# Attention, gated MLP and slot MLP in one kernel: the sums' 1e-9 as a second column, sink values split by a cast and one operation, and a set-up called later

## Chip, core and metric

The kernel runs on one core of a Trainium2 chip. The metric is device time in microseconds of one execution, launch to end. The parts of a core that matter here are TensorE (PE in the profile; PEld is its weight load), VectorE (DVE), ScalarE (ACT), GpSimd (POOL) and the queue on SyncE (SP) that issues all DMAs.

## Reference

Three layers, all in fp32, follow one another. Attention has 4 batches, 8 heads, 768 positions and 64 dimensions per head; a query sees the 4 first keys (the sinks) and the 128 keys up to itself.

```
scores = np.where(keep, scores, -1000000000.0)
scores = scores - np.max(scores, axis=-1, keepdims=True)
a = np.exp(scores)
a = a / (np.sum(a, axis=-1, keepdims=True) + 1e-09)
attn = np.matmul(a, v)                               # -> x, 3072 x 512
gate = 1.0 / (1.0 + np.exp(-(x @ w_gate)))
x = (gate * (x @ w_val)) @ w_out                     # d_ff = 1536
logits = x @ phi                                     # 8 experts x 4 slots = 32
d = softmax over the tokens; slot_input = d.T @ x
slot_out[e] = np.maximum(slot_input[e] @ w1[e], 0.0) @ w2[e]
out = softmax over the slots of logits @ slot_out    # 3072 x 512
```

## The kernel before

The 3072 tokens are worked in 8 halves of a batch (384 tokens each). A half has 4 pairs of heads, and a pair has 3 units of 128 queries, so there are 96 units. `stage_a` of a unit makes the scores on PE (L300, two heads), masks them and takes the row minimum of their negative on DVE (L304), and exponentiates on ACT (L321), which also writes the sum of each row to a column of the tile `sm` (128 x 2, one column per head). The inner function `norm` adds 1e-9 to the sums (L325), takes the reciprocal (L326), and has POOL multiply the probabilities (L327). `stage_b` transposes them on PE, `stage_c` multiplies them with the values; `sink_parts` (L339, L340) splits the sinks' probabilities into a high and a low part. Some products take a value as such a pair of parts.

`sinks(b)` does such a split for the sinks' values of batch b, once for each of the 4 batches: the tile `rv` is loaded, and `cut` makes from it, in four DVE operations on 128 x 512 elements, the tile `vs`, which holds the high part in the rows where `vsel[:, 0:1]` is 1 and the low part in the others:

```
pin(dve.tensor_copy(vh, rv))
dve.tensor_tensor(rv, rv, vh.bitcast(F32), op=ALU.subtract)
dve.tensor_scalar(rv, rv, vsel[:, 1:2], None, op0=ALU.mult)
dve.scalar_tensor_tensor(vs, vh.bitcast(F32), vsel[:, 0:1], rv, op0=ALU.mult, op1=ALU.add)
```

The MLP's weights come as 64-bit floats. In the first of five passes over them, `w_start` makes fp32 of each of 36 tiles: two operations on ACT (L513, L514), three on DVE (L517, L518, L521), one on POOL (L525), and a DMA writes it out for the later passes. `gemm1` (L632) multiplies with gate and value weights, `gemm2` (L670) with the output weights, and DVE adds the latter's result into `ysb` (L675). The first half's attention comes before the first MLP product; the attention of later halves is spread between the products, by a credit that the main loop keeps. `setup_merge` fills constants (`ones`, `R`, `dm`, `R2`) that only the end of the kernel reads.

All engines take their instructions in order. The order is not the order of the code alone: a scheduler sets it when the program is built, and only instructions under `pin` keep the code's order among themselves.

Of the kernel before, what the change touches and what calls it, by code (L numbers as in the profile page):

```python
# [9 lines left out]
F32 = mybir.dt.float32  # L10
# [5 lines left out]
ALU = mybir.AluOpType  # L16
AX = mybir.AxisListType
# [19 lines left out]
def fused_kernel(ctx, tc, qT, kA, kB, vB, vS, wg, wv, wo, phi, w1, w2, n_sink, window, out):  # L37
    nc = tc.nc
    pe, act, dve, pool, sp = nc.tensor, nc.scalar, nc.vector, nc.gpsimd, nc.sync
# [8 lines left out]
    def ps(tag, bufs, dt=F32):  # L48
        return psum.tile([128, 512], dt, name=tag, tag=tag, bufs=bufs)
# [13 lines left out]
    pin = tc.keep_in_program_order  # L63

    def setup_masks(cp):
# [34 lines left out]
        pin(dve.tensor_copy(identr, ident))  # L100

        pin(dve.tensor_reduce(vsel[:, 0:1], ident.rearrange("p (a b) -> p a b", b=16)[:, :, 0:8], axis=AX.XY, op=ALU.max))
        pin(dve.tensor_scalar(vsel[:, 1:2], vsel[:, 0:1], -1.0, 1.0, op0=ALU.mult, op1=ALU.add))
        for t in T2 + tt2:
            pool.memset(t.bitcast(F32), 0.0)

# [14 lines left out]
    vsel = per.tile([128, 2], F32, name="vsel")  # L121
# [38 lines left out]
    at = left.enter_context(tc.tile_pool(name="at", bufs=1))  # L160
# [8 lines left out]
    def later(k, fn):  # L169
        pend.append([k, fn])  # L170
# [72 lines left out]
    def run_split():  # L243
        at_tasks.popleft()[1]()
# [3 lines left out]
    def sinks(b):  # L248

        rv = at.tile([128, 4, 128], F32, name="rv", tag="rv", bufs=1)  # L250
        sp.dma_start(out=rv, in_=vS[:, 4 * b:4 * b + 4])

        def cut():
            vh = at.tile([128, 4, 128], F32R, name="vh", tag="vh", bufs=1)
            vs = at.tile([128, 4, 128], F32R, name="vs", tag="vs", bufs=2)
            pin(dve.tensor_copy(vh, rv))
            dve.tensor_tensor(rv, rv, vh.bitcast(F32), op=ALU.subtract)
            dve.tensor_scalar(rv, rv, vsel[:, 1:2], None, op0=ALU.mult)
            dve.scalar_tensor_tensor(vs, vh.bitcast(F32), vsel[:, 0:1], rv, op0=ALU.mult, op1=ALU.add)
            VS[b] = vs  # L260
        later(3, cut)

# [11 lines left out]
    def stage_a(u):  # L274
# [18 lines left out]
        else:  # L293
            P = at.tile([128, 2, 260], F32, name="P", tag="P", bufs=3)
        nb = at.tile([128, 2], F32, name="nb", tag="nb", bufs=4)
        sm = at.tile([128, 2], F32, name="sm", tag="sm", bufs=4)
        Ss = [ps("ys", 3) for h in range(2)]
        for i, k in enumerate(QK[n][1:]):
            for h in range(2):
# [19 lines left out]
            src, dst = P[:, :, 0:128], PC[n][:, jj, :, 4:132]  # L319
        for h in range(2):  # L320
            act.activation(out=dst[:, h], in_=src[:, h], func=ACTF.Exp, scale=-1.0,  # L321
                           bias=nb[:, h:h + 1], accum_out=sm[:, h:h + 1])

        def norm():
            dve.tensor_scalar(sm, sm, 1.0e-9, None, op0=ALU.add)  # L325
            dve.reciprocal(sm, sm)  # L326
            pool.tensor_tensor(dst, dst, sm.unsqueeze(2).to_broadcast([128, 2, src.shape[2]]), op=ALU.mult)  # L327
            if wide:
                act.copy(PC[n][:, jj, :, 0:4], P[:, :, sk:sk + 4])
            normed.add(u)  # L330
            if jj == 2:
                later(1, sink_parts)
# [263 lines left out]
    ops = [(si, o, i) for si in range(NS) for o, i in (LAST if si == NS - 1 else ORDER[len(steps[si][0]) - 1])]  # L596
    LA = 4
    w_due, due = {}, {}
    for k, (si, o, i) in enumerate(ops):
        ns, h = steps[si]  # L600
# [424 lines left out]
    fast = nc.values_load(flag, min_val=0, max_val=1)  # L1025
    phase[0] = 0

    setup_merge()
    credit = 0.0
    NX = [10, 5, 8]  # L1030
    xe = []
# [1 line left out]
    for k, (si, o, i) in enumerate(ops):  # L1033
        phase[0] = steps[si][0][0] // NF
        if o == "y":
            if si:
                gemm2(si - 1, i)
        else:
            gemm1(si, i, o)
        tick()  # L1040
        now[0] = k + 1
        rate = 0.0
        for h in range(NH):
            todo = half_at[h] - emitted[0] - credit
            if todo > 0 and due[h] > now[0]:
                rate = max(rate, todo / max(due[h] - (3 if h == 1 else 5) - now[0], 1))
        credit += rate
        while credit >= 1:
            credit -= 1
            attn_piece()  # L1050
        if m2:
            m2_piece()
            if si == NS - 1:
                m2_piece()
        if x_can():
            x_split()
        if at_tasks:
            run_split()
        w_slot()
        if not xe and len(tops) == 1 and ws_n[0] >= 3 * NF and not w_fly:  # L1060
            top.close()
            tops.append(top.enter_context(tc.tile_pool(name="parts", bufs=1)))
        if not xe and not pieces and xs_n[0] == NH:
            top.close()
            left.close()
            xe.append(ctx2.enter_context(tc.tile_pool(name="xe0", bufs=1, reuse_waits="tile")))
        if len(xe) == 1 and min(gdone[0], ydone[0]) >= N_LEAN - 1 and m2_done[0] == NH - 1:
            inner.close()
            xe.append(ctx2.enter_context(tc.tile_pool(name="xe1", bufs=1, reuse_waits="tile")))
        for q in range(len(xe)):  # L1070
            if 32 - len(e_order) in range(sum(NX[0:q]), sum(NX[0:q + 1])):
                e_load(e_tile(xe[q], f"e{q}", NX[q]))
                break
# [68 lines left out]
```

## Time and profile before

| | |
|---|---|
| median of 3 runs | 944.0 us (943.19 to 945.39) |
| the profiled execution | 944.22 us |
| its span, first to last instruction | 942.3 us |
| busy: PE | 898.0 us (95%) |
| busy: DVE | 598.7 us (64%) |
| busy: POOL | 475.9 us (51%) |
| busy: ACT | 372.4 us (40%) |
| mean granted clock of TensorE | 0.972 |

The profile is one execution; 1.9 us of its time lie outside its span. A share of busy time is a mean over stages that differ: what an engine does while another waits for it has to be read stage by stage. Busy time of one DVE instruction includes what it is held up after its start, and two that follow each other closely overlap by some 0.08 us in the records.

### The profile page before, as it was taken

Reading aid. Unit: us, or ns where it says so; the run is one execution under the profiler, and the core shown is the slowest. Engines: PE = TensorE matmul, PEld = TensorE weight load, DVE = VectorE, ACT = ScalarE, POOL = GpSimd, SP = SyncE. Lnnn points to the kernel's source line nnn. Section 1 sums busy time; section 2 is a strip of 40 time slices with the busy share of each in tenths; the row PEclk is TensorE's granted clock in tenths of the full one; section 3 lists DMA queues with packets and bytes.
Section 4 is the critical chain, followed back from the end, with each engine's and each line's share of the span. In section 5 each row is a group of like instructions: output and inputs, shape, how many; then the busy total and the mean of one; then the engine's idle time right before and its main releaser. Section 6 shows DMA issues by size and latency. Waiting matters only on the chain.

```text
span 942.3 us, 15253 instructions
## 1 busy us (share of the span) xinstructions
PE 898.0 (95%) x5276; PEld 712.5 (76%) x5277; DVE 598.7 (64%) x1536; ACT 372.4 (40%) x996; POOL 475.9 (51%) x428
## 2 busy tenths in 40 slices
PE   8789998989999999999999999999999999899894
PEld 4455554556789999888889999898999987798452
DVE  8996869666558757765776767766455533444532
ACT  5675565333343343344343443343332323241221
POOL 3753445463346675655675756654644422684000
PEclk7799999999999999999999999999999999999897
DMA  6884657531213232333232333231212169656997
GB/s 230 285 268 154 226 173 230 165 100 44 68 54 103 82 106 54 106 84 99 59 105 68 98 78 96 77 101 55 79 57 68 45 211 387 230 155 196 310 323 236
DMA packets 80355, 133.40 MB, mean 142 GB/s; under 512 B 6800, under 2 KB 38544, under 8 KB 80272
## 3 DMA queue, kind: packets, MB, share of 16 engines
q1 hardware_dynamic: 80272, 132.37, 46.1%
q8 instruction: 43, 0.70, 0.3%
q14 instruction: 40, 0.33, 0.1%
HBM read 116.62 MB, written 15.73 MB: 140 GB/s over the span
## 4 chain that ended last, share of the span: by engine, by line
PE 78%; DVE 8%; DMA 4%; issue 4%; ACT 3%; POOL 1%; SPq 0%; POOLq 0%; DVEq 0%; ACTq 0%
PE gv L632 39%; PE ys L670 20%; PE ys L300 4%; PE xt L392 4%; DMA wraw<-wsv 2%; PE ys L857 2%; PE pt L367 2%; DVE wA L517 2%; DVE wA L518 1%; PE ys L697 1%; PE xt L395 1%; PE ys L706 1%; DVE wA L521 1%; PE xt L878 1%; DMA wbits<-in_wv_dram 1%
## 5 line engine op out<-in xcount | busy, mean ns | idle before, releaser
L632 PE MATMUL gv<-xh,whv 128*128 128x384 f32 x432 | 151.6, 379 | 3.2 <-ACT whv L190 3.2
L632 PE MATMUL gv<-xh,whg 128*128 128x384 f32 x432 | 153.1, 383 | 0.0
L670 PE MATMUL ys<-who,gh 128*128 128x512 f32 x324 | 140.2, 460 | 7.8 <-DVE ysb L675 6.3
L649 POOL TENSOR_TENSOR gl<-th,gh 128x384 fp32r<-128x384 f32 x84 | 89.3, 1063 | 111.8 <-DVE gh L192 95.0
L675 DVE SCALAR_TENSOR_TENSOR ysb<-ys,ysb 128x512 f32<-128x512 f32 x138 | 93.0, 683 | 37.8 <-PE ys L670 37.1
L632 PE MATMUL gv<-xh,wlv 128*128 128x384 f32 x336 | 114.3, 340 | 0.7 <-POOL wlv L495 0.7
L632 PE MATMUL gv<-xl,whv 128*128 128x384 f32 x336 | 114.3, 340 | 0.0
L632 PE MATMUL gv<-xl,whg 128*128 128x384 f32 x336 | 114.0, 339 | 0.0
L632 PE MATMUL gv<-xh,wlg 128*128 128x384 f32 x336 | 113.3, 337 | 0.0
L321 ACT ACTIVATE PC<-P,nb 128x132 f32<-128x132 f32 (+1 forms) x152 | 60.2, 397 | 109.0 <-DVE P L315 77.7
L670 PE MATMUL ys<-wlo,gh 128*128 128x512 f32 x252 | 99.5, 395 | 0.0
L670 PE MATMUL ys<-who,gl 128*128 128x512 f32 x252 | 98.4, 396 | 0.0
L632 PEld LDWEIGHTS gv<-xh,whv 128*128 128x128 f32 x432 | 81.3, 190 | 20.0 <-issue 6.4
L327 POOL TENSOR_TENSOR PC<-PC,sm 128x264 f32<-128x264 f32 (+1 forms) x76 | 50.3, 663 | 90.4 <-DVE sm L326 68.3
L632 PEld LDWEIGHTS gv<-xh,whg 128*128 128x128 f32 x432 | 81.7, 191 | 16.0 <-issue 4.7
L495 POOL TENSOR_TENSOR wlv<-wraw,whv 128x512 fp32r<-128x512 f32 x48 | 63.0, 1313 | 58.6 <-ACT whv L190 54.0
L670 PEld LDWEIGHTS ys<-who,gh 128*128 128x128 f32 x324 | 60.2, 189 | 36.6 <-issue 18.2
L645 DVE SCALAR_TENSOR_TENSOR th<-th,gv 128x384 f32<-128x384 f32 x84 | 46.3, 551 | 61.4 <-PE gv L632 50.5
L495 POOL TENSOR_TENSOR wlg<-wraw,whg 128x512 fp32r<-128x512 f32 x48 | 62.5, 1302 | 34.1 <-ACT whg L190 26.9
L304 DVE CUSTOM_DVE_ANT_0 P<-ys,mask 128x260 f32<-128x260 f32 (+1 forms) x152 | 57.2, 392 | 34.1 <-PE ys L300 34.0
L636 ACT ACTIVATE th<-gv 128x384 f32<-128x384 f32 x96 | 46.8, 487 | 80.4 <-PE gv L632 79.8
L325 DVE TENSOR_SCALAR sm<-sm 128x2 f32<-128x2 f32 x96 | 35.9, 374 | 63.5 <-ACT PC L321 57.9
(211 smaller groups left out, 1834.7 us busy)
## 6 DMA issues: line engine op xcount, KB each, us to landing
ew<-in_w_dram SPq DMA_DIRECT2D x32, 1024.0 KB, 12.1
wraw<-wsg SPq DMA_DIRECT2D x48, 256.0 KB, 2.7
wraw<-wsv SPq DMA_DIRECT2D x48, 256.0 KB, 2.7
wraw<-wso SPq DMA_DIRECT2D x48, 256.0 KB, 2.7
wbits<-in_wg_dram SPq DMA_DIRECT2D x12, 512.0 KB, 4.2
wbits<-in_wv_dram SPq DMA_DIRECT2D x12, 512.0 KB, 4.6
wbits<-in_wo_dram SPq DMA_DIRECT2D x12, 512.0 KB, 4.7
out_dram<-ew SPq DMA_DIRECT2D x8, 768.0 KB, 6.8
```

Of the source, the lines that this page charges most:

```text
L300: pe.matmul(Ss[h][:, 0:w], QK[n][0][h][:, 128 * jj:128 * jj + 128], k[h][:, w0:w0 + w], start=(i == 0), stop=(i == len(QK[n]) - 2))
L304: dve.tensor_tensor_reduce(out=P[:, h, 0:w], in0=S[:, 0:w], in1=mask[:, MOFF[mt]:MOFF[mt] + w], scale=-0.125, scalar=3.0e38, op0=ALU.add, ...
L321: act.activation(out=dst[:, h], in_=src[:, h], func=ACTF.Exp, scale=-1.0, bias=nb[:, h:h + 1], accum_out=sm[:, h:h + 1])
L327: pool.tensor_tensor(dst, dst, sm.unsqueeze(2).to_broadcast([128, 2, src.shape[2]]), op=ALU.mult)
L392: pe.matmul(xt[64 * h:64 * h + 64, cols], VT[n][:, jj + s - i, 64 * h:64 * h + 64], pts[:, i, h, :], start=(jj == 0 and i == 0), stop=Fals ...
L495: pool.tensor_tensor(lo, r, hi.bitcast(F32), op=ALU.subtract)
L632: pe.matmul(acc_ps[:, 0:384], wt[:, 128 * d:128 * d + 128], xt[:, d, :], start=(k == 0), stop=(k == 4 * len(seq) - 1))
L636: act.activation(out=th, in_=acc_ps[:, 0:384], func=ACTF.Tanh, scale=0.5)
L645: dve.scalar_tensor_tensor(gr, th, 1.0, acc_ps[:, 0:384], op0=ALU.add, op1=ALU.mult)
L649: pool.tensor_tensor(gl, gr, gh.bitcast(F32), op=ALU.subtract)
L670: pe.matmul(yp, a[:, 128 * i:128 * i + 128], w, start=(k == 0), stop=(k == len(seq) * len(ns) - 1))
L675: dve.scalar_tensor_tensor(ysb[h][:, i, :], yp, 0.5, ysb[h][:, i, :], op0=ALU.mult, op1=ALU.add)
```

## The change

Four places change. The exponentials' sums go to the first column of a new tile `sm2` (128 x 2 x 2), whose second column is set to 1e-9 by a memset; `norm` adds the two columns by one reduce in place of an addition of a constant. `cut` makes the high part by a cast on ACT and `vs` by one DVE operation, `vh * (vsel0 - 1) + rv`; `vsel[:, 1:2]` becomes `vsel0 - 1`. The call of `setup_merge` moves from ahead of the main loop to a quarter of the way through it.

```
-        pin(dve.tensor_scalar(vsel[:, 1:2], vsel[:, 0:1], -1.0, 1.0, op0=ALU.mult, op1=ALU.add))
+        pin(dve.tensor_scalar(vsel[:, 1:2], vsel[:, 0:1], -1.0, None, op0=ALU.add))
...
-            pin(dve.tensor_copy(vh, rv))
-            dve.tensor_tensor(rv, rv, vh.bitcast(F32), op=ALU.subtract)
-            dve.tensor_scalar(rv, rv, vsel[:, 1:2], None, op0=ALU.mult)
-            dve.scalar_tensor_tensor(vs, vh.bitcast(F32), vsel[:, 0:1], rv, op0=ALU.mult, op1=ALU.add)
+            act.copy(vh, rv)
+            dve.scalar_tensor_tensor(vs, vh.bitcast(F32), vsel[:, 1:2], rv, op0=ALU.mult, op1=ALU.add)
...
+        sm2 = at.tile([128, 2, 2], F32, name="sm2", tag="sm2", bufs=4)
         sm = at.tile([128, 2], F32, name="sm", tag="sm", bufs=4)
+        dve.memset(sm2[:, :, 1:2], 1.0e-9)
...
-                           bias=nb[:, h:h + 1], accum_out=sm[:, h:h + 1])
+                           bias=nb[:, h:h + 1], accum_out=sm2[:, h, 0:1])
...
-            dve.tensor_scalar(sm, sm, 1.0e-9, None, op0=ALU.add)
+            dve.tensor_reduce(sm, sm2, axis=AX.X, op=ALU.add)
             dve.reciprocal(sm, sm)
...
-    setup_merge()
...
+        if k == len(ops) // 4:
+            setup_merge()
```

The scheduler orders the changed program anew. Three places follow. From `norm` on, the changed program's lines have numbers one higher (the reduce is L326, the reciprocal L327); `sm_221`, `sm_358` and the like are buffers of `sm2`.

**First place.** DVE soon after the start, in the first units' masks (L304, a row for the operation and a row `nb` for its accumulator), where the first batch's `cut` stands; before:

```order
L256 CAST vh<-rv 128x512
L326 RECIPROCAL sm<-sm 128x2
L517 TENSOR_SCALAR wA<-wA 128x512
L304 ISA PW,nb<-ys,mask 128x260
L304 ISA nb 128x1
L257 TENSOR_TENSOR rv<-rv,vh 128x512
L304 ISA PW,nb<-ys,mask 128x260
L304 ISA nb 128x1
L518 TENSOR_SCALAR wA<-wA 128x512
L325 TENSOR_SCALAR sm<-sm 128x2
```

The same stretch of DVE in the changed program:

```order
L326 TENSOR_REDUCE sm<-sm_221 128x2
L103 TENSOR_SCALAR vsel<-vsel 128x1
L305 ISA PW,nb<-ys,mask 128x260
L305 ISA nb 128x1
L327 RECIPROCAL sm<-sm 128x2
L257 SCALAR_TENSOR_TENSOR vs<-vh,vsel,rv 128x512
L297 MEMSET sm_358 128x2
L305 ISA PW,nb<-ys,mask 128x260
L305 ISA nb 128x1
L305 ISA P,nb<-ys,mask 128x128
```

Three of `cut`'s four operations are gone, the last one stands before the first weight's L517 (now L518), and each reciprocal is followed by the memset of a later unit's `sm2`. Four such memsets stand at the program's start. `cut` of the second batch, which stood far behind (second place), now stands 48 rows below this one.

ACT, a little later in the first half, where that second batch's cast now stands between exponentials (L322), weights (L514, L515) and copies of transposed probabilities (L363):

```order
L330 COPY PC<-PW 128x2x4
L363 COPY pts<-pt 128x512
L322 ACTIVATE PW,sm_393<-PW,nb 128x260 x2
L515 ACTIVATE wS<-wbits 128x512
L256 CAST vh<-rv 128x512
L330 COPY PC<-PW 128x2x4
L363 COPY pts<-pt 128x512
```

The first batch's cast is ACT's first instruction after its warm-up, ahead of all exponentials; the third's stands 19 rows below the second's; the last one comes later.

**Second place.** DVE in the first pass over the weights, between two additions into `ysb` (L675 before, L676 in the changed program); before, with the second batch's `cut`:

```order
L675 SCALAR_TENSOR_TENSOR ysb<-ys,ysb 128x512
L256 CAST vh<-rv 128x512
L518 TENSOR_SCALAR wA<-wA 128x512
L325 TENSOR_SCALAR sm<-sm 128x2
L257 TENSOR_TENSOR rv<-rv,vh 128x512
L521 SCALAR_TENSOR_TENSOR wA<-wbits,wA 128x512
L326 RECIPROCAL sm<-sm 128x2
L258 TENSOR_SCALAR rv<-rv,vsel 128x512
L517 TENSOR_SCALAR wA<-wA 128x512
L259 SCALAR_TENSOR_TENSOR vs<-vh,vsel,rv 128x512
L518 TENSOR_SCALAR wA<-wA 128x512
L304 ISA P,nb<-ys,mask 128x260
```

And in the changed program:

```order
L676 SCALAR_TENSOR_TENSOR ysb<-ys,ysb 128x512
L522 SCALAR_TENSOR_TENSOR wA<-wbits,wA 128x512
L518 TENSOR_SCALAR wA<-wA 128x512
L326 TENSOR_REDUCE sm<-sm_1412 128x2
L519 TENSOR_SCALAR wA<-wA 128x512
L327 RECIPROCAL sm<-sm 128x2
L297 MEMSET sm_1671 128x2
L522 SCALAR_TENSOR_TENSOR wA<-wbits,wA 128x512
L518 TENSOR_SCALAR wA<-wA 128x512
L519 TENSOR_SCALAR wA<-wA 128x512
L305 ISA P,nb<-ys,mask 128x260
```

All four operations of `cut` have left this place. The next addition into `ysb` follows 19 rows below the first before, and 16 rows below it in the changed program, with seven operations on weights between the two in both. The third batch's one operation stands 23 rows behind that next addition.

**Third place.** DVE at the start, where the scheduler had put `setup_merge` (L134, L135, L142) among the masks; before:

```order
L134 TENSOR_TENSOR R<-ident 96x32
L142 COPY R_77<-ident 128x16
L88 SCALAR_TENSOR_TENSOR mask<-cid,nwf,mask 128x128
L142 COPY R_77<-ident 128x16 x3
L118 TENSOR_REDUCE flm<-fl 128x1
L135 TENSOR_TENSOR R<-R,ident 96x32
L142 COPY R_77<-ident 128x16 x4
```

And in the changed program:

```order
L134 TENSOR_TENSOR R<-ident 96x32
L142 COPY R_77<-ident 128x16
L88 SCALAR_TENSOR_TENSOR mask<-cid,nwf,mask 128x128
L142 COPY R_77<-ident 128x16 x3
L118 TENSOR_REDUCE flm<-fl 128x1
L135 TENSOR_TENSOR R<-R,ident 96x32
L142 COPY R_77<-ident 128x16 x4
```

Nothing moved here, though the call stands elsewhere in the code: these instructions depend on little, and the scheduler takes them as early as before.

## Rows read from the trace of the kernel before

**Rows 1.** Windows: stretch, length, busy (x count) of PE, PEld, DVE, ACT, POOL; clock; DMA.
```profile
0.00:70.00 70.00, 57.60 (x253) 32.32 (x255) 62.70 (x206) 46.10 (x136) 37.37 (x42) 0.80 0.80 261
70.00:200.00 130.00, 122.92 (x511) 67.30 (x510) 96.97 (x230) 67.35 (x176) 62.05 (x53) 0.99 0.59 181
200.00:780.00 580.00, 580.00 (x3544) 510.04 (x3545) 374.48 (x962) 216.04 (x599) 324.00 (x291) 1.00 0.30 85
```

**Rows 2.** Waits of PE, 0 to 70 us: total, times, longest.
```profile
PE ys L300 <- DVE nb L304: 6.1, 7, 1.6
```

**Rows 3.** Waits of PE, 70 to 200 us.
```profile
PE ys L670 <- DVE ysb L675: 6.3, 3, 2.8
```

**Rows 4.** Chain that ended last, 0 to 70 us: shares, then start, length, piece.
```profile
by line: DVE wA L517 13.5%; issue 8.7%; DVE wA L518 8.2%; DVE PW L304 6.3%; ACT PW L321 6.0%; DVE wA L521 5.8%; DVE sm L325 5.5%; DMA nw<-in_window_dram 5.1%; DMA rv<-in_vS_dram 3.4%; PE gv L632 3.0%; PE ys L300 2.9%; DVE Ta L340 2.0%; ACT 
...
12.23 0.34 DVE vh L256
...
13.31 1.11 DVE rv L257
...
15.57 0.40 DVE rv L258
```

**Rows 5.** Timeline of DVE, first 7 us: start, length, instruction, idle before it.
```profile
0.83 0.06 DVE L108 MEMSET m_run<- 96x2 f32 x1
...
4.84 0.17 DVE L79 CAST nwt<-nw 128x4 f32<-128x4 int32 x1 [2.47 <-DMA nw<-in_window_dram]
...
6.62 0.15 DVE L118 TENSOR_REDUCE flm<-fl 128x1 f32<-128x4 f32 x1
```

**Rows 6.** Windows of L325 alone: its busy time and count.
```profile
0.00:66.00 66.00, 7.12 (x15) 0.79 0.81 266
```

**Rows 7.** Timeline of DVE, 26 to 42 us.
```profile
26.79 1.01 DVE L325 TENSOR_SCALAR sm<-sm 128x2 f32<-128x2 f32 x1
27.71 0.68 DVE L521 SCALAR_TENSOR_TENSOR wA<-wbits,wA 128x512 int32<-128x512 int32 x1
...
30.28 1.10 DVE L325 TENSOR_SCALAR sm<-sm 128x2 f32<-128x2 f32 x1 [0.52 <-ACT PW L321]
...
31.49 1.15 DVE L517 TENSOR_SCALAR wA<-wA 128x512 f32<-128x512 f32 x1
```

**Rows 8.** Timeline of POOL, the same stretch.
```profile
30.07 1.28 POOL L525 TENSOR_TENSOR whg<-wA,wS 128x512 int32<-128x512 int32 x1
```

**Rows 9.** Line 517 and line 325: ns min/median/max.
```profile
L517 DVE TENSOR_SCALAR wA<-wA x36: 399/427/1521, 12.6 to 169.3; 128x512 f32<-128x512 f32 x36
L325 DVE TENSOR_SCALAR sm<-sm x96: 155/170/1781, 10.5 to 735.9; 128x2 f32<-128x2 f32 x96
```

**Rows 10.** Tile rv, first 13 us: issue on SP (length; start), time to landing.
```profile
L251 SPq DMA_DIRECT2D rv<-in_vS_dram x1: 432/432/432, 3.5 to 3.5; - x1
...
DMA to landing us min/median/max: 4.3/4.3/4.3
```

**Rows 11.** Timeline of ACT, 8 to 12 us.
```profile
9.01 0.40 ACT L321 ACTIVATE PC<-P,nb 128x128 f32<-128x128 f32 x1 [6.78 <-DVE nb L304]
...
11.31 0.66 ACT L513 ACTIVATE wA<-wbits 128x512 f32<-128x512 f32 x1
```

**Rows 12.** Chain that ended last, 136 to 150 us.
```profile
138.13 1.10 DVE vh L256
...
140.73 0.59 DVE rv L257
...
142.00 0.38 DVE rv L258
...
142.72 0.07 DVE vs L259
142.80 1.53 issue
```

**Rows 13.** Timeline of PE, 136 to 152 us.
```profile
149.36 1.98 PE L670 MATMUL ys<-who,gh 128*128 128x512 f32 x4 [2.40 <-DVE ysb L675]
```

## The prediction

> **What bounds the kernel now.** I read the windows first. From 200 to 780 us PE is busy for all of 580.00 us, and no other engine for more than two thirds; from 0 to 70 us PE is busy for 57.60 us and DVE for 62.70 us, from 70 to 200 us PE for 122.92 us [rows 1]. So PE lies idle for 12.4 us in the first stretch and 7.1 us in the second, 19.5 us in all, and only what shortens these idle times shortens the kernel, because the work of PE itself is not touched by the change. The waits say whom PE waits for: first mostly DVE's masking, which sets the scores' buffers free [rows 2], later DVE's addition into `ysb`, three times and 6.3 us [rows 3]. The chain of the first 70 us runs mostly through DVE: the weights' L517, L518 and L521, the masks and, with 5.5% (3.9 us), L325, an addition on 128 x 2 elements [rows 4]. Work taken off DVE there should let PE start its full stretch earlier, by as much as the chain gets shorter.
>
> Every unit beyond 200 us has the same edits, and I cost them at nothing: PE's own work covers them, with DVE busy for 374.48 of 580 us. Were that cover gone, they would cost or bring what the same edits do early on. After 780 us no L325 is left (the last begins at 735.9 [rows 9]), and the fourth batch's `cut` comes long before that.
>
> **Part 1, the sums.** L325 took 0.17 us at the median and up to 1.78 us [rows 9]. In the first 66 us fifteen of them took 7.12 us [rows 6]; at 0.16 us each that is 2.4, so 4.7 us are time in which they were held. The rows show by what: one began at 30.28 us and took 1.10, to 31.38, and POOL's instruction that began at 30.07 and took 1.28 ended at 31.35 [rows 7, 8]. The reduce that takes its place is nearest to the row of a reduce from 4 elements to one, 0.15 us [rows 5], so without a hold it costs the same, and the question is what of the 4.7 us goes. The bounds are 0 and all of it. What speaks for little: the held L325 at 26.79 us is followed by L521 [rows 7], which would have met the same POOL instruction, as far as L521 is held too. What speaks for something: behind the one at 30.28 us, L517 was held as well (1.15 us, against a median of 0.43) [rows 7, 9]. Without the first hold L517 meets the POOL instruction that held L325, and the second hold, 0.7 us, goes. With L517, L518 and L521 making up 27.5% of the chain [rows 4], the next instruction that can be held is seldom far. I take a third, **-1.5 us**.
>
> The Trainium skill, SBUF — State Buffer (Who interferes with whom), says that DVE and GpSimd share one pair of ports, that a copy, cast or addition of a constant between SBUF tiles can hold it against GpSimd or be held, and that a reduce never contends. The row at 30.28 us agrees with the first half; no row here shows a reduce beside a busy POOL. By that rule alone the reduce is never held and the sum would be -4.7 here; the rule itself leaves open whether the next instruction is held in its stead.
>
> Against this stand 96 memsets. By the order, twenty come before the first half's attention is done, about the first 66 us. Four stand at the program's start, ahead of L79, before which DVE idles for 2.47 us until a DMA lands [rows 5]; they are hidden there. The other sixteen cost 0.06 us each by the nearest row, a memset of 96 x 2 [rows 5]: **+1.0 us**. From below the bound is 0 (they fall into idle gaps); from above it is that they are held as L325 was, 7.12 / 15 = 0.47 us each, +7.6 in all. I take the memset's own row, which ran with POOL hardly started and is all there is. No exponential waits for them: a memset follows the reciprocal of the unit four before, well ahead of its unit.
>
> **Part 2, `cut`.** For the first batch three DVE operations go: 0.34, 1.11 and 0.40 us on the chain [rows 4], 1.85 in all. The fourth keeps its size. But the order brings the second batch's one operation into the first half: 0.60 us when nothing holds it (L521 is the same kind and size, 0.68 less 0.08 of overlap [rows 7]), up to 1.60 as its forerunner needed later (0.07 and 1.53) [rows 12]; the middle is 1.1. Together **-0.75 us**, between -1.25 and -0.25.
>
> The cast goes to ACT. The first stands ahead of all exponentials. Its data were issued at 3.5 us and landed 4.3 us later, so at 7.8 to 7.9 us, and ACT idled before its first exponential at 9.01 us [rows 10, 11]; the cast, 0.66 us by the nearest row [rows 11], fits between. If the data came 1.2 us later, the exponentials behind it and all that follows them would wait. The second and third casts fall into ACT's busy stretch, 46.10 of 70 us [rows 1]: 0 if beside other work, 1.3 us if both lie on the chain. ACT's exponentials hold 6.0% of that chain [rows 4], so most of it is covered; I take **+0.3 us**. The loads of `rv` are issued earlier on SP for the second and third batch, and what is queued behind them there are weight loads and stores; they wait for one DVE operation each, which now comes early, so I add nothing.
>
> Later, at the second place, four operations leave DVE: 1.10, 0.59, 0.38 and 1.60 us on the chain, 3.67 in all [rows 12]. They stand right ahead of the 2.40 us for which PE waited for the addition into `ysb` [rows 13]. Two of them were plainly held, and holds may move on to their neighbours: unheld they are 0.34, 0.59, 0.38 and 0.60, or 1.9 us. A little later the third batch's one operation comes in, 0.6 to 1.6 us, before the last of the three waits. So DVE gains between 0.3 and 3.1 us by then; the middle, **-1.7 us**. What is late next is the same addition, at its two other waits (3.9 us together by rows 3 and 13), which shrink no further when a DMA or PE itself sets them.
>
> **Part 3, `setup_merge`.** The order shows its instructions where they were, among the first masks. The edit does nothing, 0 us: the scheduler undoes it.
>
> **Sum:** -1.5 + 1.0 - 0.75 + 0.3 - 1.7 = -2.65. The profiled execution took 944.22 us, 942.3 of them its span, and stands 0.2 us above the median of 944.0. 944.2 - 2.65 = **941.6 us**, by 0.28%. A measurement of this kernel tells about 0.2% from no change, so this is only just faster. The lower ends together give -1.25 - 4.7 + 0 + 0 - 3.1 = -9.05, or 935.2; the upper ones -0.25 + 0 + 1.0 + 1.3 - 0.3 = +1.75, or 946.0, and with held memsets 6.6 more, 952.6.
>
> **Rivals.**
> The holds vanish: none of L325's 4.7 us falls on the next instruction. For it speaks that masks and reciprocals, which read at most one tile of SBUF, often stand between; against it the pair L325 and L521 at 26.79 us. The sum becomes -2.65 - 3.2, and the time **938.4 us**. This is what the rule of the SBUF page gives if nothing is passed on.
> The relief doesn't reach PE: ACT and the DMAs (share 0.80 in the first 70 us [rows 1]) hold the chain as soon as DVE lets go of it, and the `ysb` additions are late for other reasons. Then parts 1 and 2 give nothing early, the second place its 0.3, the casts cost 0.3: **944.2 us**. For it speaks that "issue", ACT and DMAs are a good fifth of the chain's first names; against it that DVE is busy for 90% of the stretch.
> Slower: the memsets take over L325's role and are held by POOL, 0.47 us each in the first 66 us. That adds 6.6 to the sum: +3.95, or **948.2 us**. For it speaks that nothing is known of a memset beside a busy POOL in this trace, against it the same page of the Trainium skill, by whose section an instruction with at most one SBUF input outside the fast modes isn't held. It decides from a mean of 0.35 us per memset: 16 x 0.35 = 5.6 is 4.6 more than the 1.0 in the sum, which turns -2.65 into +1.9, the 0.2% that can be told.
>
> **How the numbers follow.** The forecast: 0.42, with its own range of 939.5 to 943.7 us (a term of 2 us either way). Vanished holds: 0.17. No relief: 0.25. Held memsets: 0.10. The rest, 0.06, is for the new order of thousands of rows elsewhere, of either sign. Faster by over 0.2% is below 942.3: two thirds of the forecast (0.28), all of the second (0.17), some of the third and the rest (0.08), together 0.53. Slower is held memsets, half of the rest and a fifth of no relief, 0.18. Within 0.2%: 0.29. The range of 937.0 to 946.0 leaves out the held memsets and the far ends of vanished holds and of the rest, under 0.2.
>
> **What would show it.** In the changed kernel: reduces near 0.15 us with no long ones; memsets at 0.06 us; L518, L519 and L522 held more often than L517, L518 and L521 were; PE idle in the first 70 us some 1 us shorter; the wait of PE for the addition into `ysb` that ended at 149.36 us gone or under 1 us; PE without a gap from 200 to 780 us as before; `setup_merge` in the first 9 us. The prediction is wrong if PE's idle time before 200 us shrinks by less than 1 us or by more than 5, or if a gap opens where PE has none now.

## The result: faster by 1.25%, more than four times what was predicted

The kernel after the change took 932.81 us at the median (932.42 to 934.68, 4 runs), the kernel before 944.69 us on the same chip (943.19 to 947.58, 4 runs): a ratio of 0.9875, with a 95% interval of 0.9849 to 0.9901. The prediction was 941.6 us, with a range of 937.0 to 946.0; the result is 4 us under its lower end.

The windows of the kernel after, over the stretches of [rows 1] (length, then busy time and count of PE, PEld, DVE, ACT and POOL; granted clock; DMA):

```profile
0.00:70.00 70.00, 57.06 (x248) 31.98 (x248) 59.06 (x227) 48.10 (x140) 37.25 (x43) 0.78 0.80 263
70.00:200.00 130.00, 129.50 (x564) 74.05 (x563) 99.09 (x253) 71.50 (x188) 65.99 (x55) 1.00 0.57 185
200.00:780.00 580.00, 580.00 (x3547) 512.25 (x3548) 358.44 (x1012) 214.35 (x593) 324.51 (x292) 1.00 0.31 91
```

DVE has 3.6 us less to do in the first 70 us, and PE gains nothing from it: it idles for 12.9 us there, where it idled for 12.4. The gain stands in the second row: 0.5 us of idle time where there were 7.1. PE's waits of the kernel after, first from 0 to 70, then from 70 to 200 us (total, times, longest), show what is left of [rows 2] and [rows 3]:

```profile
PE ys L301 <- DVE nb L305: 7.1, 4, 3.1
...
PE ys L301 <- DVE nb L305: 0.5, 1, 0.5
```

All three waits for the addition into `ysb` are gone, not only the one at 149.36 us. To see when the lead builds up, I read from PE's timeline when it began the n-th record of a gate or up product (L632, L633 after the change), in microseconds from the span's start:

| record | before | e1 | e2 | e7 | after |
|---|---|---|---|---|---|
| 24th | 68.34 | 68.42 | 70.45 | 67.20 | 68.99 |
| 96th | 111.58 | 111.22 | 114.22 | 110.98 | 112.75 |
| 192nd | 177.94 | 175.72 | 178.15 | 171.44 | 173.14 |
| 240th | 207.52 | 206.28 | 202.55 | 196.63 | 197.54 |
| 400th | 280.08 | 278.80 | 274.44 | 268.52 | 269.44 |
| 2000th | 806.12 | 806.52 | 800.70 | 794.59 | 795.61 |

The kernel after is 1.2 us late at the 96th record, which is within chance (see the caution below), and 10.6 us early at the 400th; nothing changes from there to the 2000th. (The other columns are experiments, told below; e1 loses 1.7 us between its last two rows, and the last section says to what.) PE has the same 978 records between the 24th and the 400th in both kernels, in another order. Of the 11.3 us by which it does it faster, 6.6 are the idle time of 70 to 200 us and 1.7 a group of L670 that ran at the low clock in the kernel before. Some 3 us lie in many small steps, which I could not assign.

The other predictions for the profile held. The reduce and the memset of the sums are short in all 96 units, none of them held (ns min/median/max):

```profile
L326 DVE TENSOR_REDUCE sm<-sm x96: 140/156/159, 10.7 to 725.4; 128x2 f32<-128x4 f32 x96
...
L297 DVE MEMSET sm<- x96: 60/60/60, 0.8 to 675.5; 128x2 f32 x96
```

The short cut's two operations, the cast now on ACT (ns min/median/max, first and last start):

```profile
L256 ACT CAST vh<-rv x4: 603/611/617, 7.8 to 163.5; 128x512 fp32r<-128x512 f32 x4
L257 DVE SCALAR_TENSOR_TENSOR vs<-vh,vsel,rv x4: 730/1515/2423, 11.8 to 315.7; 128x512 fp32r<-128x512 f32 x4
```

The Trainium skill, SBUF — State Buffer (Who interferes with whom), says that a reduce never contends with GpSimd; the trace agrees: the longest of 96 took 159 ns, with POOL busy for 37.25 of the first 70 us.

The holds (time in which a DVE instruction stood still after its start) moved to the neighbours, as forecast. Windows of 0 to 66 us in the kernel after, of L518, L519, L522 and L326 alone, one row each:

```profile
0.00:66.00 66.00, 11.29 (x14) 0.77 0.81 269
0.00:66.00 66.00, 9.88 (x13) 0.77 0.81 269
0.00:66.00 66.00, 10.38 (x13) 0.77 0.81 269
0.00:66.00 66.00, 2.13 (x16) 0.77 0.81 269
```

The same windows in the kernel before, of L517, L518 and L521 (L325 is in [rows 6]):

```profile
0.00:66.00 66.00, 11.08 (x14) 0.79 0.81 266
0.00:66.00 66.00, 8.85 (x14) 0.79 0.81 266
0.00:66.00 66.00, 8.92 (x13) 0.79 0.81 266
```

The sums lost 7.12 - 2.13 = 5.0 us, the weights' three steps gained 0.21 + 1.03 + 1.46 = 2.7 us (with one instruction fewer, 40 against 41), and twenty memsets took 1.1.

So two theories stand against each other. **Relief**: the shorter DVE work takes the waits away, whatever the order. **Order**: the scheduler answers the edits with another order of all engines, and that order takes them away.

### The profile page after: what moved, and what is told of

Its sections match the earlier page's. It is cut to its first block, busy times and chain, and to the rows that moved or that the text cites. A ratio compares the mean times of both kernels' runs of the same rounds, so it can differ in the third digit from the quotient of the medians.

```text
span 930.6 us, 15349 instructions
## 1 busy us (share of the span) xinstructions
PE 893.3 (96%) x5277; PEld 712.4 (77%) x5277; DVE 576.4 (62%) x1620; ACT 375.1 (40%) x1000; POOL 475.6 (51%) x428
## 5 line engine op out<-in xcount | busy, mean ns | idle before, releaser
L633 PE MATMUL gv<-xh,whv 128*128 128x384 f32 x432 | 151.0, 379 | 2.5 <-ACT whv L190 2.5
L633 PE MATMUL gv<-xh,whg 128*128 128x384 f32 x432 | 153.0, 383 | 0.0
L676 DVE SCALAR_TENSOR_TENSOR ysb<-ys,ysb 128x512 f32<-128x512 f32 x138 | 93.3, 685 | 38.9 <-PE ys L671 38.0
L633 PE MATMUL gv<-xh,wlv 128*128 128x384 f32 x336 | 114.6, 341 | 0.7 <-POOL wlv L496 0.7
L633 PE MATMUL gv<-xl,whv 128*128 128x384 f32 x336 | 114.1, 340 | 0.0
L633 PE MATMUL gv<-xl,whg 128*128 128x384 f32 x336 | 114.1, 340 | 0.0
L633 PE MATMUL gv<-xh,wlg 128*128 128x384 f32 x336 | 113.5, 338 | 0.0
L322 ACT ACTIVATE PC<-P,nb 128x132 f32<-128x132 f32 (+1 forms) x152 | 60.1, 396 | 91.2 <-DVE P L316 74.2
L633 PEld LDWEIGHTS gv<-xh,whv 128*128 128x128 f32 x432 | 81.6, 190 | 18.3 <-issue 4.3
L633 PEld LDWEIGHTS gv<-xh,whg 128*128 128x128 f32 x432 | 81.4, 190 | 15.6 <-issue 4.9
L496 POOL TENSOR_TENSOR wlo<-wraw,who 128x512 fp32r<-128x512 f32 x48 | 61.6, 1299 | 9.0 <-ACT who L190 7.0
```

The lines of the kernel that those rows point to most:

```text
L496: pool.tensor_tensor(lo, r, hi.bitcast(F32), op=ALU.subtract)
L633: pe.matmul(acc_ps[:, 0:384], wt[:, 128 * d:128 * d + 128], xt[:, d, :], start=(k == 0), stop=(k == 4 * len(seq) - 1))
L676: dve.scalar_tensor_tensor(ysb[h][:, i, :], yp, 0.5, ysb[h][:, i, :], op0=ALU.mult, op1=ALU.add)
```

## Experiments

A median stands beside that of the kernel before on the same chip; the ratio is that of the runs, with its 95% interval. One caution for the traces: e1, e6, e14, e15, e17 and e18 do the same instructions in the same order up to the first L670 group, and reached it between 80.05 and 82.47 us. A difference of up to 2.4 us there, in one profiled execution, means nothing.

**Order against work: e1 to e4.** In these kernels each engine's order is written out and tied, so that the scheduler can only follow it:

```diff
+    for p, q in zip(order, order[1:]):
+        tc.add_manual_dep(q, p.name, mybir.DependencyInfo(mybir.DependencyClass.NoSync, mybir.DependencyReason.DATA), reason="order")
```

e1 is the kernel after in the order of the kernel before. Memsets stand behind the reciprocal of the unit four before, and ACT's casts where ACT had time.

> Every engine's instructions stand in the order of the kernel before; both edits are in (memset and reduce for the addition, the short cut with ScalarE's cast, placed at 139.0 us for b=1). Theory A, relief: the gain of 11.7 us comes from the shorter VectorE work, whatever order the scheduler picks; then this gives 932 to 937 us. Theory B, order: the scheduler's new order of TensorE and VectorE work takes the three waits for ysb away, and the edits themselves are worth what the prediction's sum said or less; then this gives 940 to 945 us, with the waits of TensorE for ysb near 149, 173 and 196 us still there in part. In between, 937 to 940: both.

Measured: 943.98 against 943.62 us, ratio 0.9996 (0.9977 to 1.0015). In the old order the edits are worth nothing that can be told. PE's waits for `ysb` in e1 (L692 there is L670) are those of the kernel before but for the first, which is [rows 13] cut from 2.40 to 0.61 us. The other two in the kernel before (start, length, idle before it):

```profile
173.03 1.98 PE L670 MATMUL ys<-who,gh 128*128 128x512 f32 x4 [1.14 <-DVE ysb L675]
...
196.25 3.68 PE L670 MATMUL ys<-who,gh 128*128 128x512 f32 x4 [2.76 <-DVE ysb L675]
```

All three in e1:

```profile
147.20 1.98 PE L692 MATMUL ys<-who,gh 128*128 128x512 f32 x4 [0.61 <-DVE ysb L697]
...
170.81 1.98 PE L692 MATMUL ys<-who,gh 128*128 128x512 f32 x4 [1.13 <-DVE ysb L697]
193.60 2.84 PE L692 MATMUL ys<-who,gh 128*128 128x512 f32 x4 [2.81 <-DVE ysb L697]
```

Of the 2.2 us won by the 192nd record, 1.2 are left at the 240th: behind the last of these waits PE ran at the low clock for longer in e1 than in the kernel before (last section).

e2 is the reverse: the new order with the old work. The cut's four steps stand together where the kernel after has its one step; the memsets stay.

```diff
-            act.copy(vh, rv)
-            dve.scalar_tensor_tensor(vs, vh.bitcast(F32), vsel[:, 1:2], rv, op0=ALU.mult, op1=ALU.add)
+            dve.tensor_copy(vh, rv)
+            dve.tensor_tensor(rv, rv, vh.bitcast(F32), op=ALU.subtract)
+            dve.tensor_scalar(rv, rv, vsel[:, 1:2], None, op0=ALU.mult)
+            dve.scalar_tensor_tensor(vs, vh.bitcast(F32), vsel[:, 0:1], rv, op0=ALU.mult, op1=ALU.add)
...
-            dve.tensor_reduce(sm, sm2, axis=AX.X, op=ALU.add)
+            dve.tensor_scalar(sm, sm2[:, :, 0], 1.0e-9, None, op0=ALU.add)
```

> Every engine's instructions stand in the order of the kernel after; both edits are undone in their work: the sums take an addition of 1e-9 again (as long as in the kernel before when GpSimd holds it), and VectorE does the four steps of the cut again, where the kernel after has its one step. The 96 memsets stay (about 1 us of VectorE in the first 66 us). Theory A, relief: 941 to 946 us. Theory B, order: 932 to 936 us, with no wait of TensorE for ysb over 1 us between 70 and 200 us.

Measured: 940.69 us, 0.9967 (0.9953 to 0.9981). Neither theory alone: the waits for `ysb` are gone, but the long cut costs elsewhere. DVE's timeline of e2 shows the third batch's cut, four steps in a row, and behind it the mask for which PE waits:

```profile
159.51 1.49 DVE L277 CAST vh<-rv 128x512 fp32r<-128x512 f32 x1
161.03 0.69 DVE L278 TENSOR_TENSOR rv<-rv,vh 128x512 f32<-128x512 f32 x1
161.76 0.49 DVE L279 TENSOR_SCALAR rv<-rv,vsel 128x512 f32<-128x512 f32 x1
162.36 0.75 DVE L280 SCALAR_TENSOR_TENSOR vs<-vh,vsel,rv 128x512 fp32r<-128x512 f32 x1
163.03 0.42 DVE L328 CUSTOM_DVE_ANT_0 P<-ys,mask 128x260 f32<-128x260 f32 x1
```

PE's timeline and its windows right after (the clock is third from the end):

```profile
163.51 1.39 PE L324 MATMUL ys<-rk,rq 64*128 64x260 f32 x4 [2.36 <-DVE nb L328]
...
164.00:168.00 4.00, 4.00 (x9) 2.11 (x9) 4.00 (x12) 2.12 (x7) 0.11 (x1) 0.67 0.74 227
```

e3 undoes the sums alone, by the last two lines of that diff.

> The kernel after with one instruction form changed: the reduce over two columns is an addition of 1e-9 to one column again; order, memsets and the short cut stay. If the held additions cost the end (theory A, the sums' share of it): 935 to 940 us. If they do not in this order (theory B): 932 to 934 us, although the additions take 5 to 7 us in the first 66 us again instead of 2.1.

Measured: 933.08 us, 0.9886 (0.9861 to 0.9910). In the new order the held additions cost nothing, though they took 5.00 us in the first 66 us again.

e4 undoes the cut alone, by the other lines, and sets `vsel` back with it.

> The kernel after with the four steps of the cut on VectorE again, at the place of its one step, and no cast on ScalarE; memsets, reduces and the order stay. Theory A, relief: the 4 to 5 us of VectorE that come back for each of the first two batches, in the first 70 us in this order, cost 1 to 4 us: 934 to 937 us. Theory B, order: 932 to 934 us.

Measured: 939.57 us, 0.9961 (0.9938 to 0.9984). So in the new order the short cut is worth 7.6 us (e2 less e3, which ran on the same chip), and the reduce nothing. Tying the order costs nothing that shows: e3 is tied and takes the time of the kernel after.

**Each edit alone, the scheduler free: e7 and e8.** e7 is the kernel before with the new `cut` and `vsel`, e8 the kernel before with memset and reduce. (The third edit, `setup_merge`, has no run of its own; e7 is without it.)

> The short cut alone, the scheduler free to order: at the two places its TensorE order reads like that of the kernel after, with the four products of whv ahead of the twelfth L670 group. Order theory: all of the gain, 931 to 935 us, though the additions are held as before. Theory A (relief by both edits in proportion): 937 to 941 us.

> Memset and reduce alone, the scheduler free to order: at the two places its TensorE order reads like that of the kernel before. Order theory: no gain, 941 to 945 us. Theory A: 938 to 941 us.

Measured: e7 932.45 us, 0.9885 (0.9861 to 0.9909), the whole gain. e8 939.04 us, 0.9935 (0.9913 to 0.9956). That is within what Relief gave, and outside what Order gave. But the scheduler was free in e8, and PE's order there is another than in the kernel before; with the old order kept (e1), the reduce and the short cut together were worth nothing. In e8's own order PE's idle time in the first 70 us is 8.4 us; the wait at 192 us stays:

```profile
0.00:70.00 70.00, 61.61 (x268) 34.83 (x269) 62.17 (x234) 50.97 (x148) 39.33 (x44) 0.83 0.83 266
...
192.03 3.02 PE L673 MATMUL ys<-who,gh 128*128 128x512 f32 x4 [2.28 <-DVE ysb L678]
```

So the sums bring another order too, with a gain at another place; I take that order for the cause, though no run has e8's order without the sums. With the cut beside them that order is not found.

**The pin: e9 and e10.** The old cut's first step was pinned to its place in the program (`pin` is `tc.keep_in_program_order`); the new cut has no pin. The last steps of the four cuts began at 19, 143, 317 and 513 us in the kernel before, and at 12, 24, 158 and 316 us in the kernel after: from the second on, each stands about where its forerunner stood.

```diff
-            pin(dve.tensor_copy(vh, rv))
+            dve.tensor_copy(vh, rv)
```

> The kernel before with all its work, and one word taken out: the first step of the cut (L256) is no longer pinned to its place in the program, so that the scheduler may take it earlier. Fence theory: it is this pin, which the change drops with the old first step, that held the cuts of the second to fourth batch at 138, 315 and 509 us; without it they come at some 25, 160 and 320 us, the order turns to that of the kernel after, and with the long cut in it the time is that of run e2, 937 to 941 us. Theory that the shorter work makes the order: nothing changes, 942 to 945 us.

Measured: 944.90 against 944.86 us, 1.0012 (0.9991 to 1.0032). The cuts do come at 14, 27, 160 and 325 us, and the waits of L670 for `ysb` fall from 6.3 to 1.1 us, but nothing is won. PE is 2.3 us late at the 24th record, 3.2 us early at the 240th and 1.5 at the 400th. Whether the long cut in the first half costs what the later order brings is not shown: 2.3 us is within chance there, and PE's idle time of the first 70 us (12.7 against 12.4 us) hardly differs. PE's order in e9 is a third one, neither that of the kernel before nor that of the kernel after.

e10 is the kernel after with the pin on its one step:

```diff
-            dve.scalar_tensor_tensor(vs, vh.bitcast(F32), vsel[:, 1:2], rv, op0=ALU.mult, op1=ALU.add)
+            pin(dve.scalar_tensor_tensor(vs, vh.bitcast(F32), vsel[:, 1:2], rv, op0=ALU.mult, op1=ALU.add))
```

> The kernel after with one word put in: the short cut's operation on VectorE is pinned to its place in the program, as the first step of the old cut was. Memsets, reduces and the cast on ScalarE stay; the scheduler is free otherwise. Fence theory: the cuts move back to some 135, 310 and 505 us, and the gain is gone for the most part, 938 to 944 us. Theory that the shorter work is enough: 931 to 935 us.

Measured: 939.53 us, 0.9946 (0.9929 to 0.9964), the cuts at 13, 135, 308 and 503 us. That is e8's time. Pinned, the short cut adds nothing to the sums; unpinned, the long cut brings nothing (e9, without the sums). Short and unpinned, it brings 12 us without the sums (e7) and 6.7 from e10 to the kernel after.

**One place of the order: e5, e6, e13 to e16.** At 171 to 196 us the old order has a chain that reaches over five engines. In e1, ACT's cast of `qs` waits for a load ahead of one attention unit's exponentials, and DVE's cast of `kh` for another load ahead of its reciprocal; the addition for which PE waits is behind both. First ACT's rows, then DVE's:

```profile
182.95 0.83 ACT L254 CAST qs<-rqs 64x768 fp32r<-64x768 f32 x1 [4.70 <-DMA rqs<-in_qT_dram]
183.69 0.40 ACT L343 ACTIVATE PC<-P,nb 128x132 f32<-128x132 f32 x1
...
184.60 0.16 DVE L347 TENSOR_REDUCE sm<-sm 128x2 f32<-128x4 f32 x1 [4.54 <-ACT PC L343]
186.36 0.70 DVE L258 CAST kh<-rks 128x1040 fp32r<-128x1040 f32 x1 [1.60 <-DMA rks<-in_kB_dram]
...
187.31 0.16 DVE L348 RECIPROCAL sm<-sm 128x2 f32<-128x2 f32 x1
...
191.05 0.18 DVE L361 CAST Ta<-PC 128x32 fp32r<-128x32 f32 x1 [1.74 <-POOL PC L349]
...
192.87 0.68 DVE L697 SCALAR_TENSOR_TENSOR ysb<-ys,ysb 128x512 f32<-128x512 f32 x1
```

In the kernel after the same unit's exponentials stand ahead of ACT's cast, its reciprocal ahead of DVE's, and both loads land earlier:

```profile
179.82 0.40 ACT L322 ACTIVATE PC<-P,nb 128x132 f32<-128x132 f32 x1
...
182.54 0.83 ACT L233 CAST qs<-rqs 64x768 fp32r<-64x768 f32 x1 [1.85 <-DMA rqs<-in_qT_dram]
...
181.35 0.16 DVE L327 RECIPROCAL sm<-sm 128x2 f32<-128x2 f32 x1
...
184.86 1.00 DVE L237 CAST kh<-rks 128x1040 fp32r<-128x1040 f32 x1 [3.34 <-DMA rks<-in_kB_dram]
...
191.90 0.68 DVE L676 SCALAR_TENSOR_TENSOR ysb<-ys,ysb 128x512 f32<-128x512 f32 x1
```

PE's order differs too: four products of `whv` stand behind the L670 group that waited at 173 us before, and ahead of it after. e5 moves PE's work alone, in the kernel before (the second move, at 196 us, is alike):

```diff
 L632 MATMUL gv<-xh,whg 128x384
+L632 MATMUL gv<-xh,whv 128x384 x4
 L670 MATMUL ys<-who,gh 128x512 x2
 L300 MATMUL ys<-rk,rq 128x260
-L632 MATMUL gv<-xh,whv 128x384 x4
```

> The kernel before with its own work and its own order on every engine, but for two moves on TensorE: four gate-and-up products (those of whv that follow the L670 group that started at 173.03 us) stand ahead of that group, and sixteen instructions (nine gate-and-up products, five of the attention's values, two transposes) stand ahead of the L670 group that started at 196.25 us. No edit of the change is in. If the order at these places is the cause: the waits of 1.14 and 2.76 us go, and with the second the 1.7 us at the low clock, 937 to 940 us. If the addition on VectorE is late whatever stands ahead (theory of the held or late VectorE work): the waits turn up at the next group, 942 to 945 us.

> Run e1 (both edits in the old order) with the same two moves on TensorE. Order theory: e1's time less 4 to 6 us, 937 to 940 us by the runs of e1; if its trace's gain at 149 us adds, 936 us. Theory of late VectorE work: 942 to 945 us.

Measured: e5 943.73 against 944.41 us, 1.0003 (0.9985 to 1.0021); e6 942.23 us, 0.9968 (0.9949 to 0.9987), so 3.0 us, a quarter of the lead. PE's timeline of e5: the waits for `ysb` at these two places are gone, and PE waits for the attention's tiles instead, which come from the same late chain:

```profile
189.83 0.41 PE L388 MATMUL pt<-ident,PC 128*128 128x128 f32 x2 [1.62 <-DVE pts L398]
197.72 0.77 PE L413 MATMUL xt<-pts,vt 128*64 128x128 f32 x8 [2.22 <-DVE pts L398]
```

e13 moves the other engines' steps, in the kernel before; e14 does it in e1, e15 in e1 with e5's first move, and e16 undoes it in the kernel after. On ACT in e13:

```diff
-act.copy(qs[0:64], rq)
 act.activation(out=dst[:, h], in_=src[:, h], func=ACTF.Exp, ...
 act.activation(out=dst[:, h], in_=src[:, h], func=ACTF.Exp, ...
 act.activation(out=th, in_=acc_ps[:, 0:384], func=ACTF.Tanh, ...
+act.copy(qs[0:64], rq)
```

> The kernel before with its work and its order, but for three moves of steps that wait for the next pair's loads at 184 to 190 us: ScalarE's cast of qs (184.22 us) behind the two exponentials and the tanh that follow it, VectorE's cast of kh (189.02 us) behind the seven instructions that follow it, up to the addition into ysb at 191.39 us, and GpSimd's product with the sums (192.47 us) ahead of its subtractions for qs and kl. No edit of the change is in. If this place is the cause: TensorE's wait of 2.76 us at 196.25 and the 1.7 us at the low clock go, 938 to 941 us. If not: 943 to 946 us.

> Run e1 (both edits in the old order) with the same three moves. If this place is the cause: 937 to 940 us by the runs of e1, and with e1's gain at 149 us kept rather 936. If not: 942 to 945 us.

> As e14, with the four products of whv ahead of the L670 group that waited 1.14 us at 173.03 (the first of e5's moves). If the two places add: 1 us under e14, 935 to 939 us. If the first place is given back later: as e14.

> The kernel after with its work and its order, but for the three moves reversed at the same place: the cast of qs ahead of the unit's two exponentials on ScalarE, the cast of kh ahead of the unit's reciprocal on VectorE, and the product with the sums behind the subtractions for qs and kl on GpSimd. If this place is the cause: the wait for ysb before 200 us comes back, 936 to 939 us. If not: 932 to 934 us.

Measured: e13 944.52 against 943.56 us, 1.0005 (0.9985 to 1.0024); e14 943.04 us, 0.9989 (0.9974 to 1.0004); e15 941.99 us, 0.9973 (0.9948 to 0.9998); e16 933.90 us, 0.9890 (0.9873 to 0.9907). The theory of this place fails in all four; only e15 gains, 2.5 us where it wanted 5 to 9. In e13 the unit's reciprocal came at 182.30 instead of 189.97 us, and PE still waited 2.6 us. POOL's rows and DVE's say why: the next unit's product is behind the subtraction for `kl`, that behind `kh`, and my move had put `kh` behind that unit's sum.

```profile
189.45 2.59 POOL L260 TENSOR_TENSOR kl<-rks,kh 128x520 fp32r<-128x520 f32 x2 [1.55 <-DVE kh L258]
192.01 0.62 POOL L348 TENSOR_TENSOR PC<-PC,sm 128x264 f32<-128x264 f32 x1
...
192.66 0.18 DVE L360 CAST Ta<-PC 128x32 fp32r<-128x32 f32 x1 [3.34 <-POOL PC L348]
```

And in e16 no wait for `ysb` came back. So this place alone is not the cause, from either side; e13 doesn't settle it by itself, since it carries the cost of its own move.

**Stretches of the order: e17, e18, e11, e12.** Both edits; one order up to a time, the other from there on, on all engines:

```diff
-order = after
+order = before[:n] + [k for k in after if k not in before[:n]]
```

> Both edits; every engine in the order of the kernel before up to the L670 group that started at 164.26 us there, and in the order of the kernel after from there on. If the gain is made by the order of 164 to 200 us (the scores of the attention ahead of the L670 groups, and with them ScalarE's, GpSimd's and the load queue's steps): 933 to 936 us. If it needs the order before 164 us: 940 to 944 us.

> As e17, with the old order kept up to the L670 group that started at 184.36 us in the kernel before, thus past the place at 173 us where the scores stand behind a waiting L670 group. If the gain is made between 164 and 184 us: 939 to 943 us while e17 is at 933 to 936 us. If it is made after 184 us: both at 933 to 936 us.

Measured: e17 937.89 against 943.84 us, 0.9927 (0.9889 to 0.9965); e18 942.02 us, 0.9981 (0.9963 to 0.9999). With the new order from 164 us on half of the lead is left, from 184 us on almost none. But each seam, the place where one order ends and the other begins, has a stall of its own, so the two gains are lower bounds for what the later order brings. PE in e17, then in e18:

```profile
175.28 4.54 PE L654 MATMUL gv<-xh,whv 128*128 128x384 f32 x8 [2.19 <-POOL whv L547]
...
193.14 0.79 PE L322 MATMUL ys<-rk,rq 64*128 64x128 f32 x2 [2.76 <-DVE ysb L697]
```

In e17 the seam costs some 4.0 us: 2.19 of waiting, and 4.54 in place of 2.74 us at the low clock. From the 96th to the 400th record (113.48 to 275.65 us) e17 still gains 6.3 us on the kernel before; with the seam's 4.0 that is 10.3, where the kernel after gains 11.8. So by its trace most of the lead comes from the order behind 164 us. e18 waits 2.76 us and then runs at a clock of 0.50 to 0.64 until 204 us, so it does not tell what the order behind 184 us is worth.

e11 and e12 begin in e8's order, for its earlier start, and go on in that of the kernel after, by the same line with `e8` in place of `before`.

> Both edits; every engine in the order of run e8 up to the first L670 group (75.1 us there, 80.8 in the kernel after), and in the order of the kernel after from there on. Run e8 was 5.6 us ahead of the kernel after at that place. If leads of two stretches add: 926 to 930 us, faster than both kernels. If VectorE, the weights or the attention's loads set the stretch that follows, the lead is given back there: 931 to 934 us.

> As e11, with the order of run e8 kept longer, up to the seventh L670 group from 75 us on (127.4 us in e8, where it was still 5 us ahead), and the order of the kernel after from there on. If leads add: 926 to 930 us. If not: 931 to 936 us.

Measured: e11 937.73 against 944.86 us, 0.9931 (0.9907 to 0.9955); e12 932.99 us, 0.9890 (0.9860 to 0.9921). Leads don't add. In e11 PE stood 4.7 us at the seam, for masks:

```profile
82.01 1.23 PE L322 MATMUL ys<-rk,rq 64*128 64x260 f32 x2 [4.71 <-DVE nb L326]
```

e12 is 8.9 us ahead of the kernel before at the 96th record, where the kernel after is late, and only 12.9 instead of 10.6 at the 400th. No version tried is faster than the kernel after by more than a measurement tells.

## Why the prediction was wrong

- **The step that failed** is the frame of the sum: every term was priced at its place in the old order, and "the new order of thousands of rows elsewhere, of either sign" got a chance of 0.06. The runs show that the gain needs the new order, with the short cut in it (e3 and e7 have it whole). The edits in the old order: 0.9996 (e1), and its interval, -2.2 to +1.4 us, doesn't hold the -2.65 either. The new order with the old work: 0.9967 (e2). Both: 0.9875. What is "late next", "the same addition, at its two other waits", did shrink, from 3.9 us to nothing: the new order puts other work ahead of it on PE and gets the attention's steps done earlier on the other engines. Which of these steps do it is not shown. The two parts don't add up either: by the ratios, 0.4 us for the edits and 3.1 for the order, but 11.8 together.
- **The second place, -1.7 us**: right where the order is kept. The wait of 2.40 us shrank by 1.8 in e1. That about 1 us of it is given back to the clock by the 240th record was not in the sum.
- **Holds, -1.5, and memsets, +1.0**: the sizes were near. By the windows DVE lost 5.0 us, got 2.7 back as holds of the neighbours and paid 1.1 for memsets, so 2.3 for the first term. But PE's idle time of the first 70 us, forecast 1 us shorter, didn't fall; the rival without relief had that right, and e3 shows the additions worth nothing in the new order.
- **The first batches' cut, -0.75, and the casts, +0.3**: no loss could be seen from the casts; the first waited 5.5 us for its load, and ACT's exponentials had not begun. But the cut's value is not in what it takes off the first batch in the old order. It is that an early cut is cheap: in the new order the long one, its four steps in a row, costs 7.6 us (e2 less e3). By the traces 3.0 us of that stand at the 24th record (70.45 against 67.49 us) and 6.5 at the 192nd (178.15 against 171.66), behind the third batch's cut.
- **Held memsets** fell with their 60 ns. `setup_merge` was priced at 0, and e7 has the whole gain without it. PE has no gap from 200 to 780 us.
- The text named as a sign of error that PE's idle time before 200 us shrinks by more than 5 us. It shrank from 19.5 to 13.4, by 6.0.

What stays open: which few steps of the new order carry the lead. PE's alone (e5, e6), and the others' alone at one place (e13, e14, e16), do not; the most that such a move brought was 3.0 us (e6). And why e8's early start is lost when the cut is edited too was not tried.

## What to carry to other kernels

Where a scheduler makes the order, an edit has two prices: that of its work in the order that was, and that of the order that comes. Tie the old order and run the new work, then the reverse; two runs tell which of them you have. They can depend on each other, as here, so neither run alone is enough. A pin on one instruction is part of the edit: it held three cuts back by 119 to 197 us. Dropping it was worth nothing with the long cut (e9), and the short cut nothing with the pin kept (e10 against e8, both with the sums).

## What the runs showed of the hardware

After some waits of PE its granted clock fell from 1.0 to 0.5, from 2.4 to 1.2 GHz; a mean between the two is a window that holds both. In e1, windows around the wait that ended at 193.60 us:

```profile
186.00:190.00 4.00, 4.00 (x26) 2.94 (x25) 2.71 (x10) 1.72 (x5) 2.81 (x3) 1.00 0.31 100
190.00:194.00 4.00, 1.19 (x5) 0.76 (x5) 2.66 (x5) 0.15 (x1) 2.82 (x3) 1.00 0.56 133
194.00:198.00 4.00, 4.00 (x7) 1.47 (x6) 2.40 (x10) 1.77 (x8) 2.53 (x2) 0.57 0.17 49
198.00:202.00 4.00, 4.00 (x20) 3.36 (x19) 1.19 (x4) 1.09 (x3) 3.57 (x4) 0.57 0.40 101
```

Gate products that followed each other at 0.17 us before the wait (190.27 and 190.44 us) did so at 0.32 us behind it (198.33 and 198.65). At 0.57 over the last two windows, 8 us of PE's work lose, by estimate, 0.43 x 8 = 3.4 us, more than the wait itself. In the kernel before the wait of 2.76 us at 196.25 us was followed by four L670 records that took 3.68 us in place of 1.98; in e17 one of 2.19 us by eight products that took 4.54 us in place of 2.74 (the same eight in the kernel after). The wait of 2.40 us at 149.36 us in the kernel before had no such cost [rows 13].

It can differ where the work does not. Between the 1500th and the 2000th gate or up product PE's records stand in one order in all 20 traces, and have the same two waits, of 1.25 and 0.38 us. In 13 traces the clock of the 5 us behind the first wait was 1.00, and the stretch took 163.9 to 164.0 us. In the other seven (e1, e5, e6, e12, e14, e15, e16) the clock was 0.66 to 0.70, and it took 165.5 to 165.6 us. The kernel before, then e1:

```profile
798.85 0.30 PE L727 MATMUL ys<-ident,E 96*128 96x96 f32 x1 [1.25 <-ACT E L717]
...
799.61 1.06 PE L750 MATMUL ys<-ysb,ET 128*32 128x512 f32 x6 [0.38 <-ACT ET L730]
...
797.70 0.30 PE L749 MATMUL ys<-ident,E 96*128 96x96 f32 x1 [1.25 <-ACT E L739]
...
798.46 1.70 PE L772 MATMUL ys<-ysb,ET 128*32 128x512 f32 x6 [0.38 <-ACT ET L752]
```

So one profiled execution can carry some 1.6 us that belong to no work or order of PE there. The prediction priced waits by their length alone.
